# A list scheduler that may keep an engine waiting a tenth of a microsecond for a more urgent operation

## The chip, the cores and the metric

The kernel runs on one core of one Trainium2 chip. The metric is device time in microseconds of one execution, the median of three runs. An execution that the hardware profiler took is read below; its span is the time from the first to the last instruction, and its own time is a little longer than its span.

## The reference, cut to what matters

A clustered attention (16 head-batches of 768 rows, 64 wide; a row attends only to keys whose nearest centroid is the same as its own) feeds two expert layers, all in fp32.

```python
mask = q_assign[:, :, :, None] == k_assign[:, :, None, :]     # argmax over 16 centroids
scores = np.where(mask, scale * (q @ k.T), -1e9)
attn = softmax(scores)                                        # 16 head-batches, 768 x 768
x = (attn @ v)  -> (1536, 512)
x = ((x @ w1) * (x @ w2) @ w3) @ w_out                        # 512 -> 1024 -> 1024 -> 512
h = x @ w_in                                                  # 512 -> 2048
out = (h * np.clip(h + 3, 0, 6) / 6) @ w_out2                 # 2048 -> 512
```

The weights arrive as 64-bit numbers and are turned into fp32 on the chip.

## The kernel before, in words

Nothing is written down in the order in which it runs. The kernel builds a list of some 4,000 operations, each with a key, the engines on which it may run and a planned duration on each, the operations that it needs, a due time, and the ring buffers that it takes and drops. `Plan.order` then simulates the five queues (PE, ACT, DVE, POOL, DMA) with these planned durations and hands out the operations one at a time; the instructions are recorded in that order, and each engine runs its own in that order, waiting at the head of its queue when an operand is not there. Some operations (copies, subtractions, the rounding of a number into a high and a low part) may run on two or three engines; the planner takes the one on which they would end first.

For each engine the planner collects the candidates, finds the earliest start among them, and lets every candidate take part that could start at most `delta` = 0.05 us later; of these the one with the smallest due time wins. Then the engine whose winner starts first is served.

Operand precision is kept by splitting: a number is a high part (rounded) and a low part (the rest), and every product is three matmuls (high by high, high by low, low by high). The rounding and the subtraction are small operations on ACT, DVE and POOL, and they are what PE mostly waits for.

The stages, with the names that the rows use:

- **Weights.** `raw` is loaded, `c0` (`cvt`, ACT), `c1` (`cvt`, L700, POOL), `c3`, `c4`, `c5` (`cvs`, L705, L709, L713, all DVE) make fp32 of it. For `w_out` and `w3` the planner then makes `woh` (high) and `wol` (low, L180 on POOL) and the transposes `pt` (L731) with their split `wT` (L186 ACT, L183 DVE). The product `w3 @ w_out` is the matmuls `psw` (L759): eight rows of blocks of eight steps, three matmuls a step; step g of the first row needs `wol` of block g.
- **Attention**, head by head. `qs`, `ks`, `vs` are splits of the inputs. `ptqB`, `ptkB` (L352) are PE transposes, copied to `qB`, `kB` (ACT or DVE), and from there by a DMA into `qA`, `kA`. `pa` (L378) is the product with the centroids, and a chain of small DVE and POOL operations on `as` (L393 to L406) makes one-hot codes `ohs`, which PE transposes (`pto`, L367) and ACT or DVE copies into `kA` and `qA` (L186 or L228). Only then can the scores `pst` (L484) begin; a row maximum `den` (L493, DVE), the exponential `p` (L501, ACT), transposes `ptr` (L509), their split `ph` (ACT), `pl` (L183, DVE) and the product `av` (L529) follow. `prd` (L567) turns the sums for the division. Between them stand the first expert's matmuls `psab` (L821).
- **First expert, second half of the tokens** (`psx` L938, `psab` L989), from 411 us, and **second expert** (`psh` L1264, `po` L1308), from 545 us to the end. Its weights are fetched in pieces (`m_gb`) and split into `m_gB`, `m_hl`, `m_w`, `m_whl`, the low part on DVE or POOL.

Rings that bind: three PSUM banks for everything called `s` (transposes, `pa`), one buffer of codes `ohs`, two `raw`, two `cvt`, two `cvs`.

Of the kernel before, what the change touches and what calls it, by code (L numbers as in the profile page):

```python
# [22 lines left out]

ENG = ("pe", "act", "dve", "pool", "dma")
LAT = {
    ("pe", "act"): 0.2, ("pe", "dve"): 0.2, ("pe", "pe"): 0.0, ("act", "dve"): 0.155, ("act", "pool"): 0.17,
# [14 lines left out]
class Plan:  # L43
# [17 lines left out]
    def order(self):  # L61
        delta, bias = 0.05, {"dve": 0.3, "pool": -0.3}
        ops = self.ops
        left, users, src = {}, {}, {}
        for k, o in ops.items():
            left[k] = len(o[4]) + len(o[11])
            src[k] = []
            for n in o[4]:
                users.setdefault(n, []).append((k, True))
            for n in o[11]:  # L70
                users.setdefault(n, []).append((k, False))
        slots = {r: [0.0] * c for r, c in self.rings.items()}
        free = dict.fromkeys(ENG, 0.0)
        port = {"dve": 0.0, "pool": 0.0}
        ready = {k: None for k, o in ops.items() if not left[k]}
        out = []
        while len(out) < len(ops):
            cand = {e: [] for e in ENG}
            for k in ready:
                o = ops[k]  # L80
                t = 0.0
                ok = True
                for r in set(o[6]):
                    c = o[6].count(r)
                    if len(slots[r]) < c:
                        ok = False
                        break
                    t = max(t, sorted(slots[r])[c - 1])
                if not ok:
                    continue  # L90
                best = None
                for e, d in o[1].items():
                    st = max(free[e], t)
                    for end, pe in src[k]:
                        st = max(st, end + LAT.get((pe, e), 0.08))
                    if e == "pool":
                        st = max(st, port["dve"])
                    elif e == "dve" and o[10]:
                        st = max(st, port["pool"])
                    f = st + d + bias.get(e, 0.0)  # L100
                    if best is None or f < best[0]:
                        best = (f, e, st)
                cand[best[1]].append((best[2], o[5], o[9], k))
            pick = None
            for e in ENG:
                if cand[e]:
                    m = min(cand[e])[0] + delta
                    c = min((d, st, i, k) for st, d, i, k in cand[e] if st <= m)
                    if pick is None or c[1] < pick[0]:
                        pick = (c[1], c[3], e)  # L110
            if pick is None:
                raise RuntimeError(f"no operation can start after {len(out)} of {len(ops)}")
            st, k, e = pick
            o = ops[k]
            o[2] = e
            del ready[k]
            for r in o[6]:
                slots[r].remove(min(slots[r]))
            end = st + o[1][e]
            free[e] = end  # L120
            if e == "pool" or e == "dve" and o[10]:
                port[e] = end
            for r in o[7]:
                slots[r].append(end + 0.3)
            out.append(k)
            for u, data in users.get(k, ()):
                if data:
                    src[u].append((end + o[8], e))
                left[u] -= 1
                if not left[u]:  # L130
                    ready[u] = None
        return [ops[k] for k in out]
# [1283 lines left out]
```

## Time and profile before

| | us |
|---|---|
| median of 3 runs | 800.38 (800.28 to 804.17) |
| the profiled execution's own time | 800.35 |
| its span | 798.5 |
| PE busy | 769.9 |
| DVE busy | 618.3 |
| ACT busy | 507.5 |
| POOL busy | 242.5 |

Busy time is the union of an engine's instructions. A matmul's end is modelled and matmuls overlap, so a PE that is busy all the time may still be slower than its best; idle time, in contrast, is time in which PE certainly did nothing.

### The profile page before, as it was taken

To read this page: it belongs to the slowest core of one execution; us is meant where nothing else is said; L and a number is where in the kernel's file an instruction comes from. 1 tells how busy PE (TensorE), PEld (TensorE's weight loads), DVE (VectorE), ACT (ScalarE), POOL (GpSimd) and SP (SyncE) were. 2 spreads that over 40 slices of the span, in tenths; PEclk is the share of its full clock that TensorE was granted. 3 is DMA by queue.
4 is the path that set the end of the run, shared out by engine and by line. 5 is a ranking of instruction groups with operands and counts; after the bars stand their busy time and mean duration, and the time that the engine had idled before them with its cause. 6 is when DMAs were issued, how large, how long until landed. Compare 5 with 4: busy or idle time off the path is not lost.

```text
span 798.5 us, 12729 instructions
## 1 busy us (share of the span) xinstructions
PE 769.9 (96%) x4498; PEld 706.2 (88%) x4498; DVE 618.3 (77%) x1099; ACT 507.5 (64%) x1008; POOL 242.5 (30%) x286
## 2 busy tenths in 40 slices
PE   4889999999999999999999999999999999999998
PEld 4667878998889999999889999999988988988986
DVE  7879888899999987788996754668688776767742
ACT  5667877787878777677854522436566657555643
POOL 5654524534355534423221322311000110200100
PEclk9989999999999999999999999999999999999999
DMA  7444333233354442431426578674121214211102
GB/s 263 141 139 128 99 108 86 86 105 102 98 169 152 154 147 99 138 102 65 144 103 185 185 234 286 195 244 153 62 66 54 92 54 141 89 62 63 44 14 79
DMA packets 53136, 98.42 MB, mean 123 GB/s; under 512 B 4849, under 2 KB 31569, under 8 KB 51537
## 3 DMA queue, kind: packets, MB, share of 16 engines
q1 hardware_dynamic: 53072, 97.62, 38.7%
q8 instruction: 35, 0.57, 0.3%
q14 instruction: 29, 0.23, 0.1%
HBM read 73.43 MB, written 17.87 MB: 114 GB/s over the span
## 4 chain that ended last, share of the span: by engine, by line
PE 79%; DVE 8%; ACT 6%; issue 3%; DMA 3%; POOL 1%; SPq 0%; ACTq 0%; DVEq 0%; POOLq 0%
PE po L1308 17%; PE psh L1264 14%; PE psab L821 8%; PE psab L989 8%; PE pst L484 7%; PE av L529 6%; PE ptr L509 6%; PE psw L759 5%; PE psx L938 4%; PE pa L378 2%; ACT p L501 1%; DMA raw<-in_moe_w_in_dram 1%; ACT ph L186 1%; DVE pl L183 1%; DVE cvs L709 1%
## 5 line engine op out<-in xcount | busy, mean ns | idle before, releaser
L186 ACT ACTIVATE ph<-ptr 128x384 fp32r<-128x384 f32 x192 | 90.9, 487 | 50.1 <-PE ptr L509 49.3
L183 DVE TENSOR_TENSOR pl<-ptr,ph 128x384 fp32r<-128x384 f32 x192 | 102.8, 549 | 16.9 <-ACT ph L186 15.5
L493 DVE TENSOR_REDUCE den<-pst 128x1 f32<-128x768 f32 x96 | 91.2, 950 | 11.9 <-PE pst L484 9.8
L700 POOL TENSOR_SCALAR cvt<-cvt 128x512 f32<-128x512 f32 x72 | 52.2, 725 | 143.4 <-ACT cvt L186 134.6
L501 ACT ACTIVATE p<-pst,den 128x768 f32<-128x768 f32 x96 | 86.3, 899 | 13.5 <-DVE den L493 12.8
L509 PE MATMUL ptr<-id_f,p 128*128 128x128 f32 x576 | 89.9, 277 | 1.8 <-DVE pl L183 1.0
L821 PE MATMUL psab<-xT,abhl 128*128 128x384 f32 x384 | 85.8, 347 | 0.6 <-ACT asb L186 0.6
L509 PEld LDWEIGHTS ptr<-id_f,p 128*128 128x128 f32 x576 | 69.9, 142 | 9.6 <-PE pt L731 1.0
L484 PE MATMUL pst<-kB,qB 128*128 128x512 f32 x192 | 71.9, 378 | 3.8 <-ACT p L501 3.7
L186 ACT ACTIVATE cvt<-raw 128x512 f32<-128x512 f32 x72 | 48.0, 668 | 43.1 <-DMA raw<-in_moe_w_out_dram 15.9
L529 PE MATMUL av<-ph,vs 128*128 128x384 f32 x192 | 69.9, 364 | 0.1
L989 PE MATMUL psab<-xT1s,abhl 128*128 128x384 f32 x384 | 67.1, 335 | 0.0
L989 PEld LDWEIGHTS psab<-xT1s,abhl 128*128 128x128 f32 x384 | 66.5, 188 | 0.4 <-ACT asb L186 0.3
L821 PEld LDWEIGHTS psab<-xT,abhl 128*128 128x128 f32 x384 | 64.6, 189 | 1.9 <-ACT asb L186 0.9
L529 PE MATMUL av<-pl,vs 128*128 128x384 f32 x192 | 64.9, 338 | 0.8 <-DVE pl L183 0.7
L484 PE MATMUL pst<-kA,qA 128*128 128x512 f32 x192 | 65.1, 344 | 0.2 <-ACT kA L186 0.2
L705 DVE TENSOR_SCALAR cvs<-cvt 128x512 int32<-128x512 int32 x72 | 35.0, 490 | 30.2 <-DMA set<-cvs 23.8
L1286 ACT ACTIVATE tt<-m_sn,three 128x384 f32<-128x384 f32 x48 | 29.5, 617 | 42.3 <-DVE m_sn L1274 32.7
L759 PE MATMUL psw<-woh,wT 128*128 128x512 f32 x128 | 53.6, 430 | 1.0 <-ACT W L186 0.4
L186 ACT ACTIVATE m_sn<-psh 128x384 f32<-128x384 f32 x64 | 31.1, 486 | 35.4 <-PE psh L1264 35.4
L713 DVE SCALAR_TENSOR_TENSOR cvs<-cvt,cvs 128x512 int32<-128x512 int32 x72 | 52.3, 728 | 0.8
L709 DVE SCALAR_TENSOR_TENSOR cvs<-raw,cvs 128x512 int32<-128x512 int32 x72 | 51.4, 717 | 0.9
(182 smaller groups left out, 1820.5 us busy)
## 6 DMA issues: line engine op xcount, KB each, us to landing
raw<-in_moe_w_dram SPq DMA_DIRECT2D x32, 512.0 KB, 4.6
m_gb<-set SPq DMA_DIRECT2D x64, 256.0 KB, 3.2
raw<-in_moe_w_out_dram SPq DMA_DIRECT2D x24, 512.0 KB, 4.2
raw<-in_moe_w_in_dram SPq DMA_DIRECT2D x16, 512.0 KB, 4.1
set<-cvs SPq DMA_DIRECT2D x32, 256.0 KB, 2.5
abp<-abhl SPq DMA_DIRECT2D x6, 1024.0 KB, 4.6
abhl<-abp SPq DMA_DIRECT2D x6, 1024.0 KB, 7.1
qn<-in_q_dram SPq DMA_DIRECT2D x16, 192.0 KB, 2.4
```

Of the source, the lines that this page charges most:

```text
L183: nc.vector.tensor_tensor(out=out, in0=a, in1=b, op=ALU.subtract)
L186: nc.scalar.activation(out=out, in_=in_, func=AF.Copy, **kw)
L484: x = mm(out=psr[:, t, ks_], lhsT=TT["q" + nm, h][:, i, cs_], rhs=flat(TT["k" + nm, h])[:, ks_], start=st, stop=sp)
L493: done["mx", n] = [other_banks(nc.vector.tensor_reduce(out=dens[h][:, 0, c:c + 1], in_=psS[h, c], axis=AX.X, op=ALU.max, negate=True), ("S ...
L501: done["ex", n] = [other_banks(nc.scalar.activation(out=flat(p), in_=psS.pop((h, c)), func=AF.Exp, bias=d[:, 0, c:c + 1], accum_out=d[:, 1 ...
L509: nc.tensor.transpose(pt[:, blk(c)], pps[h, 3 * hf + c][:, blk(2 * s + i)], id_f)
L529: mm(out=t[:, 0:HF], lhsT=vs_t[h][:, 2 * s + i, :], rhs=x_[:, i, :], start=(s == 0 and i == 0 and n == 0), stop=(s == 2 and i == 1 and n = ...
L759: mm(out=ps, lhsT=wT[m, hf][:, a, blk(kk)], rhs=w_[hf][:, kk, :], start=(g == 0 and n == 0), stop=(g == J1 - 1 and n == 2))
L821: mm(out=ps[:, 0:HF], lhsT=s[:, w, a, blk(kk)], rhs=xT0[0][:, x_, kk, hf * HF:hf * HF + HF], start=(kk == 0 and n == 0), stop=(kk == KD - ...
L989: mm(out=ps[:, 0:HF], lhsT=s[:, w, a, blk(kk)], rhs=x[:, x_, kk, hf * HF:hf * HF + HF], start=(kk == 0 and n == 0), stop=(kk == KD - 1 and ...
L1264: mm(out=ps[:, 0:HF], lhsT=left(p, l, a, kk), rhs=x[:, x_, kk, :], start=(st and kk == 0 and m == 0), stop=(kk == 1 and m == 2), skip_grou ...
L1308: mm(out=outs[b, c], lhsT=g[:, a, blk(c % 3)], rhs=w[:, w_, :], start=(first and a == 0 and w_ == 0), stop=(last and a == 1))
```

## The change

The planner gets a third rule. When the winner of an engine has been found, other candidates with a smaller due time are looked at that could start after the 0.05 us limit, but before the winner would have ended and within 0.15 us of the limit, less 0.1 us. If there are any, the one that starts first takes the winner's place, and the engine idles until it can start. In numbers: a more urgent operation may be waited for when it starts at most 0.1 us after the earliest candidate, in the planner's own time.

```diff
+WAIT = 0.15
 ENG = ("pe", "act", "dve", "pool", "dma")
...
                 if cand[e]:
                     m = min(cand[e])[0] + delta
                     c = min((d, st, i, k) for st, d, i, k in cand[e] if st <= m)
+
+                    end = min(c[1] + ops[c[3]][1][e], m + WAIT)
+                    x = [(d, st, i, k) for st, d, i, k in cand[e] if st < end - 0.1 and d < c[0]]
+                    if x:
+                        c = min(x, key=lambda x: (x[1], x))
                     if pick is None or c[1] < pick[0]:
                         pick = (c[1], c[3], e)
```

No operation is added or removed. What changes is the order on every engine, and for some operations the engine. Lines of the kernel after the change have numbers that are 6 higher.

On DVE, at the program's start, this stands between the product with the centroids of the first head (`as` from `pa`) and the first scores. Before:

```order
L393 TENSOR_REDUCE as_259<-pa 128x192
L395 TENSOR_REDUCE as_260<-as_259 128x12
L705 TENSOR_SCALAR cvs<-cvt 128x512
L397 TENSOR_TENSOR as_259<-as_259,as_260 128x192
L709 SCALAR_TENSOR_TENSOR cvs<-raw,cvs 128x512
L713 SCALAR_TENSOR_TENSOR cvs<-cvt,cvs 128x512
L395 TENSOR_REDUCE as_260<-as_259 128x12
L402 TENSOR_TENSOR ohs<-as_259,as_260 128x6x16
L705 TENSOR_SCALAR cvs<-cvt 128x512
L404 TENSOR_TENSOR as_259<-as_259,as_260 128x96
L709 SCALAR_TENSOR_TENSOR cvs<-raw_166,cvs 128x512
L183 TENSOR_TENSOR wT<-pt,wT 128x512
```

and after:

```order
L711 TENSOR_SCALAR cvs<-cvt 128x512
L719 SCALAR_TENSOR_TENSOR cvs<-cvt,cvs 128x512
L715 SCALAR_TENSOR_TENSOR cvs<-raw,cvs 128x512
L399 TENSOR_REDUCE as_262<-pa 128x192
L401 TENSOR_REDUCE as_263<-as_262 128x12
L403 TENSOR_TENSOR as_262<-as_262,as_263 128x192
L719 SCALAR_TENSOR_TENSOR cvs<-cvt,cvs 128x512
L401 TENSOR_REDUCE as_263<-as_262 128x12
L189 TENSOR_TENSOR wT<-pt,wT 128x512
L408 TENSOR_TENSOR ohs<-as_262,as_263 128x6x16
L711 TENSOR_SCALAR cvs<-cvt 128x512
L410 TENSOR_TENSOR as_262<-as_262,as_263 128x96
```

Two steps of a weight's conversion moved ahead of the codes, and the split `wT` moved ahead of the code step that writes `ohs`.

On PE, at the same place, the order before is

```order
L731 MATMUL pt<-id_f,cvs 128x128 x4
L367 MATMUL pto<-id_r,ohs 48x128 x6
L759 MATMUL psw<-woh,wT 128x512
L759 MATMUL psw<-wol,wT 128x512
L759 MATMUL psw<-woh,wT 128x512
L484 MATMUL pst<-kB,qB 128x512
```

and after

```order
L737 MATMUL pt<-id_f,cvs 128x128 x4
L765 MATMUL psw<-woh,wT 128x512
L765 MATMUL psw<-wol,wT 128x512
L765 MATMUL psw<-woh,wT 128x512
L373 MATMUL pto<-id_r,ohs 48x128 x6
L358 MATMUL ptkB<-id_r,ks 128x128 x3
L490 MATMUL pst<-kB,qB 128x512
```

The first step of `psw` went ahead of the first head's code transposes, and three transposes of the second head's keys went ahead of the first scores.

On PE, some 60 rows on, where the first head ends, the second head's scores begin and the third head is prepared, before:

```order
L509 MATMUL ptr<-id_f,p 128x128 x3
L352 MATMUL ptkB<-id_r,ks 128x128 x3
L567 MATMUL prd<-id_f,den 6x128
L509 MATMUL ptr<-id_f,p 128x128 x3
L378 MATMUL pa<-cT,qB 128x32 x6
L378 MATMUL pa<-cT,kB 128x32 x6
L759 MATMUL psw<-woh,wT 128x512
L759 MATMUL psw<-wol,wT 128x512
L759 MATMUL psw<-woh,wT 128x512 x2
L759 MATMUL psw<-wol,wT 128x512
L759 MATMUL psw<-woh,wT 128x512
L367 MATMUL pto<-id_r,ohs 48x128 x6
```

and after, ending at the same `pto`:

```order
L765 MATMUL psw<-woh,wT 128x512
L765 MATMUL psw<-wol,wT 128x512
L765 MATMUL psw<-woh,wT 128x512
L515 MATMUL ptr<-id_f,p 128x128 x6
L535 MATMUL av<-ph,vs 128x384
L535 MATMUL av<-pl,vs 128x384
L535 MATMUL av<-ph,vs 128x384
L535 MATMUL av<-pl,vs 128x384
L765 MATMUL psw<-woh,wT 128x512
L765 MATMUL psw<-wol,wT 128x512
L765 MATMUL psw<-woh,wT 128x512
L373 MATMUL pto<-id_r,ohs 48x128 x6
```

The two `psw` steps that stood in a pair (blocks 5 and 6 of `wol`) are now apart and earlier, and `ptqB`, `ptkB` and `pa` of the third head are gone from this place; they stand behind the second head's first scores now.

Over the whole program the engine changes for some operations. Of the copies of `qB`, `kB`, `qA`, `kA` DVE makes 21 instead of 29 and ACT 107 instead of 99; of the low parts and sums of the second expert DVE makes seven fewer and POOL seven more.

## Rows read from the trace of the kernel before

**Rows 1.** The page: busy time of each engine, its share of the span, instructions.

```profile
PE 769.9 (96%) x4498; PEld 706.2 (88%) x4498; DVE 618.3 (77%) x1099; ACT 507.5 (64%) x1008; POOL 242.5 (30%) x286
```

**Rows 2.** Stretches: us, busy PE, PEld, DVE, ACT, POOL, granted clock, DMA share, GB/s.

```profile
22.80:29.70 6.90, 4.80 (x26) 3.30 (x26) 6.08 (x11) 3.49 (x9) 2.84 (x4) 1.00 0.73 166
29.70:33.10 3.40, 3.40 (x15) 3.10 (x15) 3.12 (x5) 2.92 (x6) 2.95 (x4) 0.50 0.02 5
33.10:46.70 13.60, 9.24 (x57) 6.98 (x57) 13.19 (x27) 10.93 (x23) 7.79 (x10) 1.00 0.38 115
46.70:53.60 6.90, 6.90 (x31) 6.15 (x31) 4.51 (x10) 1.94 (x5) 3.54 (x5) 0.51 0.43 123
60.00:411.00 351.00, 343.66 (x2280) 314.39 (x2279) 310.36 (x584) 268.40 (x575) 149.50 (x174) 1.00 0.38 116
411.00:545.00 134.00, 133.83 (x770) 132.98 (x768) 87.59 (x134) 53.20 (x91) 33.39 (x34) 1.00 0.68 214
545.00:785.00 240.00, 239.83 (x1194) 215.63 (x1194) 169.08 (x282) 142.52 (x258) 25.72 (x17) 1.00 0.21 69
```

**Rows 3.** Timeline, first head's codes and scores: start us, us, instruction, idle before.

```profile
15.82 0.29 DVE L402 TENSOR_TENSOR ohs<-as,as 128x96 fp32r<-128x96 f32 x1
...
17.42 0.83 PE L367 MATMUL pto<-id_r,ohs 128*48 128x128 f32 x6 [0.66 <-POOL ohs L406]
17.43 0.69 DVE L183 TENSOR_TENSOR wT<-pt,wT 128x512 fp32r<-128x512 f32 x1 [0.20 <-ACT wT L186]
...
18.04 1.55 POOL L180 TENSOR_TENSOR ks<-kn,ks 128x384 fp32r<-128x384 f32 x1
...
19.44 0.63 PE L484 MATMUL pst<-kB,qB 128*128 128x512 f32 x1
...
20.72 0.92 PE L352 MATMUL ptkB<-id_r,ks 128*128 128x128 f32 x6
```

**Rows 4.** Timeline of PE, 39 to 55 us, where the second head begins.

```profile
39.44 0.39 PE L759 MATMUL psw<-woh,wT 128*128 128x512 f32 x1
...
40.36 0.72 PE L352 MATMUL ptqB<-id_r,qs 128*128 128x128 f32 x6
...
45.35 0.45 PE L352 MATMUL ptkB<-id_r,ks 128*128 128x128 f32 x3 [1.66 <-ACT kB L186]
...
47.13 1.44 PE L378 MATMUL pa<-cT,qB 128*128 128x32 f32 x6
...
52.40 0.84 PE L367 MATMUL pto<-id_r,ohs 128*48 128x128 f32 x6
...
54.34 0.40 PE L484 MATMUL pst<-kB,qB 128*128 128x512 f32 x1
```

**Rows 5.** The same stretch on DVE and POOL: last conversion step, low parts 5 and 6.

```profile
42.85 0.65 DVE L713 SCALAR_TENSOR_TENSOR cvs<-cvt,cvs 128x512 int32<-128x512 int32 x1
...
44.19 0.69 DVE L713 SCALAR_TENSOR_TENSOR cvs<-cvt,cvs 128x512 int32<-128x512 int32 x1
...
45.32 2.50 POOL L180 TENSOR_TENSOR wol<-cvs,woh 128x512 fp32r<-128x512 f32 x2
```

**Rows 6.** Groups of DVE, ACT and POOL: busy us, mean ns, idle before.

```profile
L183 DVE TENSOR_TENSOR pl<-ptr,ph 128x384 fp32r<-128x384 f32 x192 | 102.8, 549 | 16.9 <-ACT ph L186 15.5
L493 DVE TENSOR_REDUCE den<-pst 128x1 f32<-128x768 f32 x96 | 91.2, 950 | 11.9 <-PE pst L484 9.8 <-ACT cvt L186 1.2
...
L228 DVE CAST kB<-ptkB 128x384 fp32r<-128x384 f32 x8 | 4.4, 550 | 0.2
...
L186 ACT ACTIVATE kB<-ptkB 128x384 fp32r<-128x384 f32 x24 | 11.6, 490 | 5.6 <-PE ptkB L352 5.5
...
L183 DVE TENSOR_TENSOR m_whl<-m_gb,m_whl 128x512 fp32r<-128x512 f32 x7 | 4.8, 687 | 0.3 <-ACT m_whl L186 0.3
...
L180 POOL TENSOR_TENSOR m_whl<-m_gb,m_whl 128x512 fp32r<-128x512 f32 x5 | 7.1, 1427 | 57.6 <-ACT m_whl L186 29.2 <-DVE tt L1290 14.3 <-DVE m_gB L183 14.1
```

**Rows 7.** One line's instructions on DVE: shortest, median, longest ns.

```profile
L562 DVE TENSOR_SCALAR den<-den x16: 153/170/1457, 42.6 to 396.0; 128x6 f32<-128x6 f32 x16
```

## The prediction

> **What bounds the kernel now.** I read the page first: PE is busy 769.9 us, 96% of the span, and no other engine more than 77% [rows 1]. So the question is where PE is not busy, or slow. The windows by stage answer it. From 411 to 545 us PE idles 134.00 - 133.83 = 0.17 us, and from 545 to 785 us 0.17 us as well, at full clock [rows 2]. An order in which PE has no gap can't be improved by another order of the same matmuls, so the last 390 us can only stay or get worse. From 60 to 411 us PE idles 351.00 - 343.66 = 7.3 us, while DVE is busy 310.36 of 351 us, 88% [rows 2]: here the two are nearly in balance, and part of PE's waiting is for DVE. What is left is the start. Between 22.8 and 53.6 us PE idles 2.1 us, then runs 3.4 us at a granted clock of 0.50, then idles 13.60 - 9.24 = 4.4 us, then runs 6.9 us at 0.51 [rows 2]. The half clock is the level of 1.2 GHz; work done there costs twice, so these two stretches lose about 1.7 and 3.4 us. In both cases the clock fell behind a stretch in which PE had waited a third of the time. The reader should see three budgets: some 11.6 us lost at the start, 7.3 us in the attention, next to nothing after it.
>
> **The change, part by part.** The rule lets an engine wait 0.1 us at most in the planner's time, but each such choice moves all that follows. What it does must therefore be read from the order at places where PE waits.
>
> *First head.* On DVE two conversion steps now stand ahead of the codes, and `wT` ahead of L402. Now L402 begins at 15.82 us; `wT` on DVE waited for its ACT copy even so, and ran at 17.43 [rows 3]. Behind it L402 would begin at 17.43 + 0.69 = 18.1, 2.3 us later, unless the conversion that feeds `wT` is also earlier: two of its three DVE steps were moved ahead, so I take 1 us of the 2.3 back. The code transposes `pto` then come at 17.42 + 1.3 = 18.7 us. On PE `psw` is moved ahead of `pto` and fills that wait: the 1.2 us that it takes now between the end of `pto` at 18.25 and the scores at 19.44 are gone from there. The scores `pst` still need the copies of the codes, and three `ptkB` transposes (half of the 0.92 us at 20.72) now stand ahead of them; these need the POOL subtraction `ks`, which ends at 18.04 + 1.55 = 19.6 [rows 3], later if POOL does its code step first. Together I put the first scores 1.0 us later: bounds 0 (the conversion is early enough) and 2.3 us (nothing of it is). Queued behind it on PE is everything of the first head. **+1.0 us.**
>
> *Second head.* Before, PE does `ptqB`, `ptkB` and `pa` of the third head from 40.36 us on, waits for their copies (1.66 us at one of them), and reaches the pair of `psw` only behind `pa`, `pto` at 52.40 and the second head's first scores at 54.34 [rows 4], all from 46.7 on at half clock. In the new order `psw` of block 4, now at 39.44, is done earlier, and `psw` of block 5 stands in its place: PE is there at about 40 us, `ptr` and `av` and block 6 behind it, then `pto`. Block 5 needs `wol`, which POOL made as a pair from 45.32 to 47.82 us, after DVE's L713 had ended at 43.50 and 44.88 [rows 5]. In the new order DVE does the conversion of both blocks with two `pl` (549 ns each) and one row maximum (950 ns) fewer ahead of them [rows 6], 2.05 us earlier. So block 5 is ready not at 45.32 + 1.25 = 46.6 but at about 44.5 us, block 6 at 45.7, `pto` behind its `psw` at 46.4. The scores follow `pto` now after 1.94 us; ACT has one more copy between in the new order (490 ns), so they come at about 48.9 instead of 54.3: 5.4 us earlier. What was jumped over must still be done: `ptqB` 0.7, `ptkB` 0.8 and `pa` some 1.3 us at full clock, 2.8 us. Net 2.6 us, taken as **-2.5 us**; bounds -5.4 (the moved work fits into gaps behind) and 0. While PE waits for block 5, `ptr` and `av` of the first head's end wait too, and DVE's `pl` behind them.
>
> A rule speaks against this part. What the rows show is that the clock fell to half behind 4.4 us of waiting in 13.6 us [rows 2]; the new order has as much waiting in one piece. The Trainium skill (TensorE: Matmul & The Clock Gate, "HAM oscillation — how this bites in real kernels") says that gaps in PE's work let the gate throttle the clock again; this trace agrees with it twice, and by the rule this order keeps the stretch at half clock. I count the 3.4 us as lost before and after, so it is not in the sum.
>
> *Attention.* DVE makes eight copies fewer of `qB`, `kB`, `qA`, `kA`. One takes 550 ns on DVE and 490 ns on ACT [rows 6]: DVE loses 4.4 us of work, ACT gains 3.9 us. ACT is busy 268 of 351 us [rows 2] and hides them. Of the 4.4 us at most all is on the path, at least nothing; PE idles only 7.3 us in the stage for all reasons, so I take a third, **-1.5 us**.
>
> *Second expert.* Seven low parts move from DVE to POOL, at 1427 ns instead of 687 ns [rows 6]: 7 x 0.74 = 5.2 us if each were on the path, nothing if the prefetch covers it. With 0.17 us of PE idle in 240 us [rows 2] it is covered now, and POOL is busy there 25.72 us; I take **0**, bounds 0 and +5.2. If that cover went, `psh` would wait.
>
> *Ports.* A tiny instruction, L562, takes 153 ns at best and 1457 ns at worst [rows 7]: now and then it stands behind something on another engine. The new order changes which ones collide. With 16 of them, of which the median is 170 ns, I take 0, bounds -2 and +2 (one or two such waits of 1.3 us come or go). The Trainium skill (SBUF — State Buffer, "Who interferes with whom") has DVE and GpSimd share a port pair under an exclusive lock; by that rule the seven low parts on POOL could hold DVE up for as long as they run, 10 us by the row, in a stage in which DVE is idle 71 us of 240: the sum stays.
>
> The sum is +1.0 - 2.5 - 1.5 = -3.0 us. The profiled execution took 800.35 us (span 798.5), as good as the median of 800.38, so the forecast is 800.35 - 3.0 = **797.4 us**.
>
> **The rivals.** *More gain (faster).* If the scores of the second head come 5.4 us earlier and nothing of the moved work costs (2.9 us more), and DVE's relief counts in full (2.9 us more), the time is 797.4 - 5.8 = 791.6 us; if the clock also stays up, 3.4 us less. For it: DVE is idle 6.9 - 4.51 = 2.4 us in the half-clock stretch and ACT 5.0 us [rows 2], so the serial stretch on PE does starve them. Against it: the rest of the attention is in balance, and what is won early can be lost to DVE behind.
>
> *The moved step waits (slower).* PE now stands at block 5 of `psw` from about 40 us. If `wol` comes no earlier than now, at 46.6 us, PE is stopped 6.5 us with the first head's last `ptr` and `av` behind it, and the work that PE now does between 40.36 and 46.6 us (some 3.6 us beside its waits) comes later. The 2.5 us are lost, 3.6 are added, and a second half-clock stretch of the size already seen adds up to 3.4: 797.4 + 9.5 = 806.9 us. It decides from the point where block 5 is 3 us later than I reckon (47.5 us). For it: the chain before `wol` has five steps on four engines. Against it: the order of DVE, where the chain is longest, moved in its favour.
>
> *The order changes, the time does not.* From the fourth head on, counted in the planner's operations, the first scores of a head shift on PE by no more than five places either way. If the early moves cancel, 800.4 us. This is the upper middle of my own forecast's range.
>
> **How the numbers follow.** 0.5% of the median is 4.0 us, about what tells a change from none. The forecast with its bounds, 796.4 to 804.4 us, the third rival within it: 0.42. More gain: 0.37, most of it close below 796. The moved step, or any other wait like it: 0.21. Faster 0.37, same 0.42, slower 0.21. For 8 in 10 the range runs from 791 to 805 us: below it lies the gain with the clock kept up, above it the full price of the waiting step; the forecast's own range is 796.4 to 801.
>
> **What would show it.** The first `pst` at 20 to 21 us instead of 19.44; the second head's first `pst` near 49 instead of 54.34; PE idle from 60 to 411 us below 7.3 us and DVE busy there some 4 us less; no new idle on PE after 411 us. The prediction is wrong if `psw` of block 5 holds PE beyond 47.5 us, if a stretch at half clock is new or missing, or if PE idles behind 411 us.

## The result, and the profile after

The change makes the kernel slower. The median over six runs is 806.37 us (804.96 to 807.56), against 800.38 us (799.62 to 804.17) for the kernel before on the same chip: ratio 1.0066, 95% interval 1.0049 to 1.0082. The ratios in this document go by all runs of both kernels and not by the two medians alone, which here would give 1.0075. The profiled execution took 805.24 us with a span of 803.5 us. Line numbers of the kernel after are six higher than before (L709 is L715).

The page of the kernel after, its busy row, which answers to [rows 1]: POOL has 15.6 us more, the others hardly change.

```profile
PE 769.3 (96%) x4498; PEld 706.0 (88%) x4498; DVE 620.5 (77%) x1084; ACT 510.2 (63%) x1016; POOL 258.1 (32%) x293
```

Groups of the kernel after, which answer to [rows 6] and [rows 7]: the low parts `m_whl` on DVE and POOL, and the tiny instruction on the denominators.

```profile
L186 POOL TENSOR_TENSOR m_whl<-m_gb,m_whl 128x512 fp32r<-128x512 f32 x9 | 13.0, 1440 | 75.1 <-ACT m_whl L192 59.5 <-DVE tt L1296 15.7
...
L568 DVE TENSOR_SCALAR den<-den 128x6 f32<-128x6 f32 x16 | 8.1, 507 | 0.7 <-ACT p L507 0.6
...
L189 DVE TENSOR_TENSOR m_whl<-m_gb,m_whl 128x512 fp32r<-128x512 f32 x3 | 2.1, 685 | 0.0
```

Stretches of the kernel after (us, busy PE, PEld, DVE, ACT, POOL, granted clock, DMA share, GB/s), which answer to [rows 2]:

```profile
40.00:43.30 3.30, 2.46 (x9) 2.01 (x9) 3.30 (x8) 1.44 (x4) 1.35 (x3) 0.54 0.00 0
43.30:53.60 10.30, 8.43 (x53) 6.65 (x52) 9.81 (x19) 8.42 (x18) 7.59 (x9) 0.98 0.38 123
...
60.00:411.00 351.00, 345.95 (x2312) 318.29 (x2311) 314.10 (x581) 272.05 (x585) 157.20 (x174) 1.00 0.38 117
...
411.00:545.00 134.00, 129.91 (x748) 129.29 (x747) 81.77 (x126) 48.55 (x84) 29.35 (x34) 1.00 0.65 210
545.00:785.00 240.00, 237.51 (x1169) 213.34 (x1170) 170.65 (x276) 143.61 (x260) 36.30 (x23) 0.99 0.22 71
```

Up to 411 us the change does good: PE idles 5.1 us from 60 us on instead of 7.3, and of the two stretches at half clock one, 3.3 us long, is left in this execution. The last product of the attention starts at 399.7 us instead of 403.1, so 3.4 us of gain are in hand. Behind 411 us PE now idles 4.09 + 2.49 = 6.6 us, where it idled 0.34. Three stretches (PE alone) show where:

```profile
540.00:546.87 6.87, 1.20 (x8) 0.89 0.51 175
546.87:551.43 4.56, 4.36 (x12) 0.50 0.34 83
551.43:560.00 8.57, 8.57 (x44) 0.95 0.39 113
```

PE stops for 5.7 us at 541.2 us and then runs 4.6 us at a granted clock of 0.50, the 1.2 GHz level. PE's timeline of the kernel after names who ends the wait: the first copies `m_sn` of the second expert, on ACT.

```profile
538.95 2.25 PE L1270 MATMUL psh<-m_x,m_gB 128*128 128x384 f32 x12
546.87 2.29 PE L1270 MATMUL psh<-m_x1b,m_gB 128*128 128x384 f32 x6 [5.67 <-ACT m_sn L192]
549.35 2.29 PE L1270 MATMUL psh<-m_x1b,m_gB 128*128 128x384 f32 x6 [0.20 <-DVE m_sn L1280]
```

ACT's timeline, same kernel, says why `m_sn` is late: it stands in ACT's queue behind a conversion copy `cvt` whose raw weights have not landed.

```profile
536.00 0.48 ACT L192 ACTIVATE x2f<-psx 128x384 f32<-128x384 f32 x1
543.20 0.66 ACT L192 ACTIVATE cvt<-raw 128x512 f32<-128x512 f32 x1 [6.72 <-DMA raw<-in_moe_w_out_dram]
543.76 1.25 ACT L192 ACTIVATE m_gB<-m_gb 128x1280 fp32r<-128x1280 f32 x1
544.92 0.61 ACT L192 ACTIVATE m_w<-m_gb 128x512 fp32r<-128x512 f32 x1
545.44 0.47 ACT L192 ACTIVATE x2f<-psx 128x384 f32<-128x384 f32 x1
545.81 0.62 ACT L192 ACTIVATE m_hl<-m_gb 128x512 fp32r<-128x512 f32 x1
546.33 0.48 ACT L192 ACTIVATE m_sn<-psh 128x384 f32<-128x384 f32 x1
```

These `cvt` copies belong to the *set conversions*: 32 blocks of the second expert's weights (`conv_ops`, key "set") that are loaded raw, copied by ACT (step c0), clamped by POOL (c1), finished by DVE (c3 at L711, c4 at L715, c5 at L719), stored, and later fetched as `m_gb`. Their first load is issued at 358 us; they have two raw buffers, and c4 gives a raw buffer back to the next load. The last load was issued at 536.03 us; before, at 533.61 us, when PE was later by 3.9 us. The queue of SP at the end of the chain, in the kernel after and in the kernel before, and ACT's copy in the kernel before:

```profile
534.27 0.89 SPq L1166 DMA_DIRECT2D m_gb<-set  x2
536.03 0.33 SPq L687 DMA_DIRECT2D raw<-in_moe_w_out_dram  x1
```

```profile
533.61 0.33 SPq L681 DMA_DIRECT2D raw<-in_moe_w_out_dram  x1
...
536.00 0.87 SPq L1160 DMA_DIRECT2D m_gb<-set  x2
```

```profile
536.96 0.68 ACT L186 ACTIVATE cvt<-raw 128x512 f32<-128x512 f32 x1 [0.45 <-DVE cvs L705]
```

So the late issue is less than half of it. The copy is 6.2 us later than before, the issue 2.4; the copy starts 7.2 us behind its load's issue, before 3.4 us. In the kernel after two fetches `m_gb` stand just ahead of this load on the queue of SP, in the kernel before they come behind it. The kernels below part the same way: with the fetches just ahead (e1, e6, e7) the copy starts 5.8 to 5.9 us behind the issue, in all others at most 4.3. That the fetches are what holds the load up was not tested by itself.

ACT takes its queue strictly in order here. The Trainium skill, TensorE: Matmul & The Clock Gate, "Architectural detail: the array is 16× 32×32, not 1× 128×128", says so too, and this trace agrees: `m_sn` could run when PE stopped at 541.2 us, and starts at 546.33, behind five others.

The 8.8 us between the gain of 3.9 us that PE still has at 539 us and the loss of 4.9 us that it has from 601 us on are, to within 0.2 us, 5.87 us of waiting, some 2.7 us of half clock (4.56 x 0.50 + 8.57 x 0.05) and one wait of 0.42 us at 589 us. So the question for the experiments is why the conversions are late when PE is early.

### The profile page after: what moved, and what is told of

Same layout as the page of the kernel before. It is cut to its first block, busy times and chain, and to the rows that moved or that the text cites. A ratio compares the mean times of both kernels' runs of the same rounds, so it can differ in the third digit from the quotient of the medians.

```text
span 803.5 us, 12683 instructions
## 1 busy us (share of the span) xinstructions
PE 769.3 (96%) x4498; PEld 706.0 (88%) x4498; DVE 620.5 (77%) x1084; ACT 510.2 (63%) x1016; POOL 258.1 (32%) x293
## 4 chain that ended last, share of the span: by engine, by line
PE 77%; DVE 10%; DMA 5%; issue 3%; ACT 3%; POOL 1%; SPq 0%; DVEq 0%; ACTq 0%; POOLq 0%
PE po L1314 16%; PE psh L1270 14%; PE pst L490 8%; PE av L535 7%; PE psab L827 7%; PE ptr L515 7%; PE psw L765 5%; PE psab L995 4%; PE psx L944 4%; DMA raw<-in_moe_w_out_dram 3%; DMA set<-cvs 2%; PE pa L384 2%; DVE cvs L715 2%; DVE cvs L719 1%; DVE den L499 1%
## 5 line engine op out<-in xcount | busy, mean ns | idle before, releaser
L189 DVE TENSOR_TENSOR pl<-ptr,ph 128x384 fp32r<-128x384 f32 x192 | 103.6, 550 | 15.3 <-ACT ph L192 13.7
L515 PE MATMUL ptr<-id_f,p 128*128 128x128 f32 x576 | 87.7, 275 | 2.7 <-DVE pl L189 2.2
L711 DVE TENSOR_SCALAR cvs<-cvt 128x512 int32<-128x512 int32 x72 | 33.4, 471 | 31.4 <-DMA set<-cvs 16.2
L715 DVE SCALAR_TENSOR_TENSOR cvs<-raw,cvs 128x512 int32<-128x512 int32 x72 | 54.2, 757 | 0.9
L719 DVE SCALAR_TENSOR_TENSOR cvs<-cvt,cvs 128x512 int32<-128x512 int32 x72 | 52.8, 738 | 0.9
```

The source lines that it names most:

```text
L189: nc.vector.tensor_tensor(out=out, in0=a, in1=b, op=ALU.subtract)
L515: nc.tensor.transpose(pt[:, blk(c)], pps[h, 3 * hf + c][:, blk(2 * s + i)], id_f)
```

## The experiments

A choice is one operation taken by the planner, counted from 0 to 4,053. All kernels below are the kernel after with one condition or number changed, unless said otherwise.

### First four: where the rule does harm

```diff
-                    if x:
+                    if x and len(out) < 2300:              # e1_head
+                    if x and len(out) >= 2300:             # e2_tail
+                    if x and c[3][1] != "set":             # e3_setfree
+                    if x and 2300 <= len(out) < 2500:      # e4_four
```

> The rule holds only for the first 2,300 of 4,054 choices, which ends inside the last head and before the first choice in which a step of the set conversions is passed over. Theory holds (the passed-over set steps put the conversion chain back, and PE waits for it at 547 us): chain and PE both come about 3.4 us earlier, last set load issued near 530 us, no PE wait behind 540 us, 797 us. Theory shift (the earlier end of the attention alone changes how set steps and other work of DVE and ACT meet, no passed-over step is needed): last set load near 536 us as in the changed kernel, PE waits 4 to 6 us near 547 us, 804 to 806 us. Theory ports (POOL's seven more low parts in the second expert cost it): 797 us, since the rule is off there.

Measured: 806.79 us, ratio 1.0067 (1.0045 to 1.0088). No set step was passed over, and yet the last set load is 5.1 us late and PE waits 6.94 us at 548.22 us. The theory that passed-over steps alone do it falls; "shift" gives the right number.

> The rule holds only from choice 2,300 on: order before that as in the kernel before. Theory holds: set chain 3 to 5 us late as in the changed kernel while PE comes at its old time, PE waits some 3 to 5 us near 547 us, 803 to 806 us. Theory shift: chain within 1 us of the kernel before, 800 to 801.5 us. Theory ports: 805 us or more, with the loss behind 560 us and no wait near 547 us.

Measured: 806.13 us, 1.0059 (1.0037 to 1.0082), the last set load 4.7 us later than before (1.1 us of it are a later start of this execution, by its first scores), PE waiting 2.91 us at 550.00 us. Here passed-over steps do cost, without any gain ahead of them. Behind that wait 1.6 us more are lost, at 590 to 631 us.

> The rule everywhere, but a step of the set conversions that would be taken is taken and never passed over. Theory holds: chain 3 to 4 us earlier than in the kernel before, as PE, no wait near 547 us, 796 to 798 us. Theory shift: the steps still meet other work at other times, chain late by 2 us or more, 802 to 806 us. Theory ports: 805 us.

Measured: 802.82 us, 1.0018 (1.0003 to 1.0034). The time is one that "shift" allows, the mechanism half of each: the chain is 1.2 us earlier at its last load than before, but PE is 3.1 us earlier and waits 2.22 us at 544.20 us. ACT's `m_hl` there starts at 541.08 us in this kernel and also in the kernel before: here the chain's end had not moved, PE had. So the kernel before had almost no slack at this place: its `m_sn` was done at 544.85 us, and PE began the products that need it at 544.95 us.

> The rule for choices 2,300 to 2,499 alone: four choices change, of which three pass over a set step. Theory holds in its narrow form (these three put the chain back): 803 to 805 us with a PE wait near 547 us. Theory shift: within 1 us of the kernel before, 800 to 801 us, since nothing ahead comes earlier. Theory ports: 800.4 us.

Measured: 804.14 us, 1.0032 (1.0017 to 1.0048): the median says that these choices cost 2.9 us by themselves. The profiled execution, the fastest of the twelve, took 801.04 us and shows no wait of PE there, so its trace can't say where the median loses them.

### Next four: one choice, and the chain itself

The order behind the first choice that differs shows a thing that none of the theories had: in e1 the rule's last effective choice is number 2,277, where PE in the last head takes a transformed block of the first expert (`ab`) ahead of a transpose.

```diff
-                    if x:
+                    if x and len(out) < 2275:              # e5_upto2275
+                    if x and len(out) == 2277:             # e6_one_choice
```

> The rule ends two choices earlier than the one choice on PE that e1 has in the last head (a transformed first-expert block ahead of a transpose); behind it the order of every engine is that of the kernel before. Theory gap (that one choice lets the last head's row maximum come earlier on DVE, and the conversion step L715 of the set conversions, which ran in the gap ahead of it, loses its place until the head is over): chain and PE both 3 to 3.5 us earlier throughout, last set load at 530 us, no wait near 547 us, 797 us, median ratio 0.996. Theory shift (the gain ahead alone is enough to make the chain late): 804 to 807 us as in e1.

Measured: 798.38 us, 0.9966 (0.9951 to 0.9982). Without that one choice (the limit lies two numbers ahead of it) the time is 8.4 us less than in e1. The chain is ahead by 2.8 us at its last load, and PE has no wait behind 540 us (busy PE, PEld, DVE, ACT, POOL):

```profile
411.00:540.00 129.00, 127.20 (x733) 126.57 (x732) 81.83 (x128) 49.65 (x84) 30.62 (x33) 1.00 0.67 216
540.00:560.00 20.00, 20.00 (x108) 18.78 (x107) 14.64 (x25) 13.36 (x26) 2.96 (x2) 1.00 0.33 106
560.00:790.00 230.00, 230.00 (x1141) 206.36 (x1140) 158.47 (x263) 134.54 (x243) 22.71 (x15) 1.00 0.20 66
```

The 1.8 us idle ahead of 540 us are two waits for the 1 MB loads `abhl<-abp`, of which PE in the kernel before had none.

> The kernel before with the rule for that one choice alone. Theory gap: the set load that stood at 390.3 us comes 8 us later, the last one 3 to 7 us later, PE waits for it near 547 us: 804 to 808 us although nothing else is changed. Theory shift: 800 to 801 us.

Measured: 809.02 us, 1.0104 (1.0081 to 1.0127). One choice out of 4,054 makes the kernel before slower by 8 us, more than the whole change does. DVE in the kernel before, in the last head:

```profile
389.12 0.41 DVE L705 TENSOR_SCALAR cvs<-cvt 128x512 int32<-128x512 int32 x1
389.56 0.69 DVE L709 SCALAR_TENSOR_TENSOR cvs<-raw,cvs 128x512 int32<-128x512 int32 x1
390.20 0.96 DVE L493 TENSOR_REDUCE den<-pst 128x1 f32<-128x768 f32 x1
```

And DVE in e6:

```profile
388.96 0.41 DVE L711 TENSOR_SCALAR cvs<-cvt 128x512 int32<-128x512 int32 x1
389.53 0.96 DVE L499 TENSOR_REDUCE den<-pst 128x1 f32<-128x768 f32 x1 [0.16 <-PE pst L490]
390.41 0.55 DVE L189 TENSOR_TENSOR pl<-ptr,ph 128x384 fp32r<-128x384 f32 x1
390.87 1.22 DVE L189 TENSOR_TENSOR Whl<-W,Whl 128x1024 fp32r<-128x1024 f32 x1
...
400.09 0.68 DVE L715 SCALAR_TENSOR_TENSOR cvs<-raw,cvs 128x512 int32<-128x512 int32 x1
```

Before, step c4 (L709) ran at 389.56 us in a gap of 0.7 us, while the scores for the last row maximum `den` were not yet done on PE. The one choice lets PE finish those scores 0.7 us earlier (at 389.43 instead of 390.09 us), the row maximum takes the gap, and behind it the last head's work, more urgent throughout, leaves no gap for 10 us. With c4 the raw buffer is held, and with the buffer the next load on the queue of SP; in the kernel before and in e6:

```profile
390.32 0.33 SPq L681 DMA_DIRECT2D raw<-in_moe_w_out_dram  x1
...
404.38 0.38 SPq L681 DMA_DIRECT2D raw<-in_moe_w_in_dram  x1
...
446.54 0.33 SPq L681 DMA_DIRECT2D raw<-in_moe_w_out_dram  x1
```

```profile
400.84 0.35 SPq L687 DMA_DIRECT2D raw<-in_moe_w_out_dram  x1
...
404.36 0.38 SPq L687 DMA_DIRECT2D raw<-in_moe_w_in_dram  x1
...
456.12 0.33 SPq L687 DMA_DIRECT2D raw<-in_moe_w_out_dram  x1
...
540.40 0.86 SPq L687 DMA_DIRECT2D raw<-in_moe_w_out_dram  x1
```

A delay of 10.5 us at 390 us (the 6th set load) is 6.8 us at the last load, but it is not carried there as a number of microseconds. The 7th load is issued at 404.36 us, no later than before; the 15th, at 442.15, is 2.6 us earlier than before; the 16th, at 456.12, is 9.6 us later, behind a stretch from 443 to 454 us in which DVE does other work (`m_x`, `x2f`, `m_x1b`) and no conversion step. What is lost is a turn: when such a stretch begins, one block less is done. The kernel after and e9 below, which differ only in the due time of this c4, show it: from the 6th on, each set load of the kernel after stands within 1.2 us of the load with the next number in e9 (398.48 beside 399.15 us, and at the end 531.46 beside 531.27). A lost turn can also be won back. e3, in which no set step is passed over, lost the same gap (its 6th load comes at 397.23 us), and its 12th load, at 425.82 us, is 5.1 us ahead of the kernel after.

At the end of the chain in e6 PE waits 5.60 us, as in the kernel after:

```profile
542.15 2.25 PE L1270 MATMUL psh<-m_x,m_gB 128*128 128x384 f32 x12
550.00 2.29 PE L1270 MATMUL psh<-m_x1b,m_gB 128*128 128x384 f32 x6 [5.60 <-ACT m_sn L192]
```

The kernel after has the same pair: its DVE goes from L711 at 385.76 us to the row maximum, and c4 comes at 397.73 us.

For the other two kernels the order stays, and the clamp c1 is left out of the set conversions, in the kernel after (e7) and in the kernel before (e8):

```diff
         def c_clamp(e):
+            if key[0] == "set":
+                return
```

> The changed kernel in its own order, with the clamp on POOL (L706) left out of the 32 set conversions, so that each is shorter by that step and its hand-over. If the chain of set conversions is what PE waits for: no wait near 547 us, PE keeps the 3.4 to 3.9 us that it is ahead at 403 us, 796 to 797.5 us. If PE's wait has another cause: 804 to 806 us.

Measured: 802.26 us, 1.0009 (0.9992 to 1.0027): by the ratios 0.57% below the kernel after, half of what the chain theory asked for. In the profiled execution PE's wait for `m_sn` shrinks from 5.67 to 2.66 us (at 545.73 us), but PE came 1.9 us later there, so only 1.1 us of that are the chain's; the last load is issued 0.3 us sooner. The clamp is 0.74 us of a round in which the load alone takes up to 7 us. The direction is that of the chain; the size of the cut was misjudged. How much of the 0.57% is the chain's is seen with e8.

> Control: the kernel before in its own order, with the same clamp left out. Chain theory: its last conversion has some slack already in the profiled execution, so 799.5 to 800.5 us, and the spread of its executions above that (up to 805) narrows if it comes from the same wait. If the clamp itself costs time otherwise (shared ports): below 799 us.

Measured: 799.09 us, 0.9977 (0.9962 to 0.9992). Its 12 runs lie between 797.3 and 801.0 us, where the kernel before has 798.5 to 804.8 in 29. The median lies between the two forecasts (799.5 to 800.5 by the chain, below 799 by the ports) and decides for neither. Part of the scatter of the kernel before may be this same wait; no trace here shows that. As a control it says that leaving out the clamp is worth 0.23% in a kernel whose trace has no such wait of PE. Of the 0.57% of e7 that leaves some 0.34% for the wait.

### Last four: the rest of the change, and a better version

```diff
-        op(("c4",) + key, ..., due=due - 1.1,
+        op(("c4",) + key, ..., due=0.0 if key == ("set", 1, 1) else due - 1.1,   # e9_gap_back
...
-                    if x:
+                    if x and not 2275 <= len(out) < 2500:  # e10_not_four
+                    if x and len(out) < 420:               # e11_start
+                    if x and 100 <= len(out) < 1600:       # e12_second_on
```

> The changed kernel with one number altered: the conversion step L715 of set (1, 1), the one that lost its gap in the last head, is given an early due time, so that it is taken as soon as it is ready. Theory gap: the set load that stood at 390.3 us goes back to about 387 us, the chain stays ahead of its old times, PE's wait near 547 us goes, 797 to 800 us (the other passed-over steps may cost up to the 3 us that four choices alone did). If the other passed-over steps are as bad: 803 to 806 us.

Measured: 801.10 us, 1.0001 (0.9985 to 1.0018), some 1 us above the 797 to 800 of "gap". The due time of one conversion step takes back 0.65%, nearly all of the change's price: the last set load is 2.3 us earlier than before, and PE waits 0.68 us for `m_sn` instead of 5.67.

> The rule everywhere but in choices 2,275 to 2,499, where the last head meets the set conversions. Theory gap, with nothing else at fault: as e5, 798 to 799 us. If the later choices (a hold of a store step of the first expert's second half, seven more low parts on POOL) cost something of their own: 800 to 802 us, with PE waits behind 545 us.

Measured: 802.83 us, 1.0019 (1.0005 to 1.0033), so 0.53% above e5. The later choices have a price of their own. The profiled execution is the fastest of the twelve. PE's waits from 411 to 790 us in this kernel:

```profile
PE po L1314 <- ACT m_whl L192: 1.5, 1, 1.5
PE po L1314 <- DVE m_gv L189: 0.4, 1, 0.4
PE psh L1270 <- DVE tt L1296: 0.4, 1, 0.4
```

PE is 3.0 us ahead at 542 us and 0.25 us behind at 601 us, with the last set load 6 us early. Which of the later choices does it was not tried.

> The rule for the first 420 choices alone, that is the first two heads. By the prediction's own terms: +1.0 for the first head and -2.5 for the second, without the 1.5 of the later attention: PE 1.5 us ahead at 403 us, 799 us. If the later choices of the attention carry the gain: PE within 0.5 us of the kernel before at 403 us, 800 to 801 us. If the start carries all of it: 3 us ahead, 798 us.

Measured: 798.06 us, 0.9954 (0.9937 to 0.9970). PE is 4.3 us ahead at 403 us: the choices of the first two heads carry all of the attention's gain.

> The rule for choices 100 to 1,599 alone: not in the first head's start and not where the last head meets the set conversions, nor behind it. If the first head's loss is a term of its own (first scores 1.7 to 2.7 us later in the kernels with the rule there), the first scores are back at 19.4 us and its 1.7 us or more are kept to the end: 4.5 to 6 us ahead of the kernel before at 403 us, 795 to 796.5 us. If it is hidden by the second head's waits: 798 us as e5 and e11.

Measured: 795.30 us (792.99 to 798.55), 0.9930 (0.9907 to 0.9953): faster than both kernels. The first scores start at 20.5 us, those of the second head at 49.2 us, PE is 6.2 us ahead at 403 us and 6.4 us ahead at 786 us, with nothing lost behind 411 us:

```profile
60.00:411.00 351.00, 346.13 (x2309) 318.13 (x2309) 315.55 (x584) 270.59 (x582) 152.70 (x172) 1.00 0.38 118
411.00:545.00 134.00, 133.82 (x768) 132.82 (x767) 86.11 (x136) 55.31 (x95) 31.98 (x34) 1.00 0.68 217
545.00:780.00 235.00, 235.00 (x1169) 211.38 (x1168) 164.89 (x274) 138.86 (x252) 24.41 (x16) 1.00 0.20 65
```

## Why the prediction was wrong, point by point

**What bounds the kernel.** That the last 390 us could "only stay or get worse" was right, and it was where the time went. The error was to read PE's 0.17 us of idle [rows 2] as a cover. It said that nothing had been late in that execution, not by how much. The slack at the first `m_sn` was 0.1 us (e3 above).

**The step that failed: the second expert, "I take 0".** The term measured 8.8 us. Its bounds (0 to +5.2 us) came from seven low parts on POOL alone. The set conversions, which run under the first expert and feed the second, were in no term, because in the kernel before nothing waits for them. In the profile after they and the entry to the second expert cost those 8.8 us. Three things add up to that. c4 of set (1, 1) loses its gap, and the chain a turn, worth 0.65% (e9 against the change), or 1.04% alone (e6). The rule passes over set steps; e2 and e4 show a price for that, 0.3 to 0.6%, in kernels in which PE is not early. And the later choices cost 0.53% (e10 against e5). With e5's -0.34% for the attention, 0.65 and 0.53 give +0.84% against the measured +0.66%, so the parts don't simply add. That PE does not wait twice for what is late at once would explain it; it is not shown.

**First head, +1.0 us.** 21.11 us against 19.44, so +1.7 in the two traces. The start scatters by a microsecond: in the six kernels whose order there is the old one the first scores lie at 19.4 to 20.6 us (mean 20.1), in the eight with the new one at 21.1 to 22.1 (mean 21.5). That makes +1.4: sign right, size near the middle of its bounds.

**Second head, -2.5 us net.** The first scores come at 51.64 us instead of 54.34, 4.4 us earlier counted from the first head's scores (5.4 was forecast). PE's timeline of the kernel after, which answers to [rows 3] and [rows 4]:

```profile
21.11 0.76 PE L490 MATMUL pst<-kB,qB 128*128 128x512 f32 x1
...
45.10 0.49 PE L765 MATMUL psw<-woh,wT 128*128 128x512 f32 x1 [0.40 <-ACT woh L192]
46.46 0.50 PE L765 MATMUL psw<-wol,wT 128*128 128x512 f32 x1 [0.87 <-POOL wol L186]
...
51.64 0.40 PE L490 MATMUL pst<-kB,qB 128*128 128x512 f32 x1
```

The moved work came back as reckoned: the lead of 2.7 us is a lag of 0.5 at 74 us (3.2 us for the 2.8 of the sum). Net that is 1.2 us, half of the forecast. What was not reckoned is the clock. The stretch at half clock from 46.7 us on [rows 2], counted as "lost before and after", is gone in this execution, and a shorter one at 40 us remains. The order alone does not decide that: e7 and e9 have the same order there, and from 42 to 52 us they show a granted clock of 0.55 and 0.66, where the kernel after has 0.92.

**Attention, -1.5 us.** From 74 to 381 us the lag of 0.5 us turns into a lead of 3.4, so 3.9 us where 1.5 were forecast. The eight copies did leave DVE (29 to 21). But in e11 nine leave it without any choice of the rule behind the second head, so copies and start were not told apart. The sum at 403 us was -3.0 by forecast and -3.4 by the traces; its parts were less right than their total, and that the total fits is in part luck. In the seven kernels with this order of the attention the lead lies between 1.4 and 3.7 us.

**Ports, 0.** The 16 tiny instructions of [rows 7] took 7.5 us in all before and 8.1 after. Right. In the second expert DVE is busy 170.65 us instead of 169.08 with six instructions fewer, so the others took a little longer; why is not shown. Besides `m_sn`, PE's one wait for DVE from 411 to 790 us is 0.42 us, for `m_gv`, which L189 makes.

**The rivals.** "The moved step waits" gave 806.9 us, nearly the time measured, by a mechanism that happened only in small. Its condition was met: `wol` of block 5 came no earlier than before, at 46.4 us (46.6 before, 44.5 by forecast), as POOL in the kernel after shows.

```profile
45.13 1.28 POOL L186 TENSOR_TENSOR wol<-cvs,woh 128x512 fp32r<-128x512 f32 x1 [3.70 <-ACT woh L192]
```

But PE got to block 5 at 44.7 us and not at 40, so it waited 0.40 and 0.87 us there and not 6.5; the product with `wol` starts at 46.46 us, 1.0 us short of the 47.5 us at which this rival decides. The sign it named last, PE idle behind 411 us, is the one that came true.

## What to carry to other kernels

An engine that never waits for a producer says nothing about how late that producer may be. Before counting a stage as covered, follow its feeding chain back to the buffer that paces it, and read the time between the chain's last step and its first use; here that was 0.1 us, behind some 180 us of a chain with two buffers. A rule that favours urgent work in a list scheduler takes the small gaps in which low-priority steps live, and one such step, 0.7 us long, cost a turn of its chain and, 150 us later, 8 us. A scheduling rule is best tried in pieces along the order: the same rule, kept out of the start and of the crossing of the stages (e12), gains 0.7% instead of losing it.

## What the runs showed of the hardware

Short waits can bring the half clock, and not all do. In e3 a wait of 2.22 us, behind 2.25 us of matmuls, was followed by twelve matmuls in 3.88 us, which take 2.27 us in e5; the granted clock of these 3.88 us was 0.56. In e9 a wait of 0.68 us at the same place and in e10 one of 1.54 us at 549.9 us left it at 1.00. PE in e3:

```profile
539.73 2.25 PE L1270 MATMUL psh<-m_x,m_gB 128*128 128x384 f32 x12
544.20 3.88 PE L1270 MATMUL psh<-m_x1b,m_gB 128*128 128x384 f32 x12 [2.22 <-ACT m_sn L192]
```

The granted clock reads 1.00 in the kernel's first microseconds, although the matmuls run there at the pace of the half clock: in the kernel after, matmuls of 512 columns that follow one another start 0.43 us apart between 26.83 and 28.53 us (27.25, 27.68, 28.11), and 0.24 us apart at 30.11 and 30.35. In the kernel before the last such slow one starts at 21.99 us, and in e5, with the order of the kernel after, at 23.42. There the starts are to be read instead of the column.
